# Stage-1 DFT of batches two to seven as float32r products, with inputs copied through a DRAM buffer

## Chip, cores and metric

The kernel runs on one core of a Trainium2 chip. The metric is the device time of one execution in microseconds. The engines are called by the profile's names: PE multiplies matrices, DVE, ACT and POOL (GpSimd) work on elements, and SP only issues DMAs here. Sixteen DMA engines carry the transfers of all queues.

## What is computed

A long convolution along the sequence (by a real FFT of 3008 points, a product with a filter, and the inverse), and behind it a two-layer network whose activation is a rational function:

```python
X = np.fft.rfft(x, axis=1)                    # x: (8, 3008, 256)
y = np.fft.irfft(X * F[None], n=3008, axis=1)
h = y.reshape(24064, 256) @ w_in              # (256, 2048)
P = a[0] + a[1]*h + a[2]*h**2 + a[3]*h**3
Q = 1.0 + abs(b[0])*abs(h) + abs(b[1])*h**2
out = (P / (Q + 1e-6)) @ w_out                # (2048, 256)
```

## The kernel before, in words

**The network.** The 24064 positions are cut into 47 tiles of 512, and each tile into 16 units of 128 hidden channels: 752 units. A unit has six matmuls into its hidden tile h_u (lines 459 to 462), five instructions on ACT, four on DVE and two on POOL, which give a number's upper part hi_u and lower part lo_u, and six matmuls of these with the second weights (lines 536 to 538). All twelve take float32r operands, a format that one matmul multiplies at once but that holds fewer bits than float32; three such products, upper by upper, lower by upper and upper by lower, stand for one product of float32 numbers.

**The convolution.** 3008 = 47 x 64. For each batch, stage 1 multiplies by the 47-point DFT matrix a1_sb (line 300), in eight quarters q of two products j each, 96 rows by 512 columns in float32. ACT evacuates a product to tile ev (names s1e), and one DMA per quarter stores it to DRAM (scr1). Tile ev has two buffers, so the evacuation of quarter q waits until the store of quarter q - 2 is done. Stage 2 loads it back in another order, multiplies by the 64-point DFT (products y, line 348), by the filter on DVE and POOL (lines 355 to 372), and by the inverse (products z, line 381), and stores to scr2. Stage 3 loads chunks tl of scr2, five columns at a time, and does the inverse 47-point DFT (products x, line 426), whose result is split into xh and xl, the network's input.

**Order.** Each engine takes its instructions in the order in which they are written. The function pipeline writes one unit per step i. Batch zero is done ahead of it; the other batches are a generator conv_items that the steps advance: it yields a cost in us of PE's time before each product, and a step takes one item when the saved credit (RATES, 0.6 per step for batch one, then 0.38) is above zero. A bare yield inside an item leaves its rest to a later place or step. Stage 1 has one bare yield per item, and so goes to the next item in the next step if the credit allows. Stage 3 takes precedence, and a chunk whose time has come before its batch is done runs the rest of the batch's generator at once (line 694).

The order of PE, ACT, DVE and POOL is that of the writing throughout. SP's is so only up to the first unit; after that the framework's scheduler places SP's DMAs, ahead of their place in the writing where nothing that they depend on holds them. Every DMA takes one of eight completion semaphores in turn and waits for the DMA that had it before.

Of the kernel before, what the change touches and what calls it, by code (L numbers as in the profile page):

```python
# [9 lines left out]
F32 = mybir.dt.float32  # L10
F32R = mybir.dt.float32r
I32 = mybir.dt.int32
U32 = mybir.dt.uint32
AF = mybir.ActivationFunctionType
ALU = mybir.AluOpType
# [9 lines left out]
NH = 32  # L25
K2 = 24
R1 = 96
C = 256
# [6 lines left out]
XF = 1  # L35
RING = dict(a=4, w=3, q=5, hi=5, lo=4)
GAP = 4
PGAP, XGAP = 1, 1
CPOS = 3
OG = 2  # L40
# [2 lines left out]
EV1, EV2, EVO = "A", "AV", "AV"  # L43
XB, FB = 4, 3
# [12 lines left out]
TT = 512  # L57
# [45 lines left out]
def conv_moe(ctx: ExitStack, tc: tile.TileContext, xp, fr, fi, w_in, w_out, ab, mats, small, sgn, outT):  # L103
    nc = tc.nc
    B = xp.shape[0]

    consts = ctx.enter_context(tc.tile_pool(name="consts", bufs=1))
    dram = ctx.enter_context(tc.tile_pool(name="dram", bufs=3, space=DRAM))
    conv = ctx.enter_context(tc.tile_pool(name="conv", bufs=2))
# [9 lines left out]
    xh = xl = None  # L119
    mats_sb = consts.tile([128, 3, 128], F32, name="mats_sb")  # L120
    small_sb = consts.tile([R1, R1 + GE], F32, name="small_sb")
    a1_sb, e_sb = small_sb[:, :R1], small_sb[:, R1 : R1 + G]
    words = consts.tile([128, 128], F32, name="words_sb")
    sgn_sb, ab_sb, abs_sb, cf_sb = words[:, :K2], words[:, 32:44], words[:, 64:76], words[:, 96:120]
    flag_sb = words[:, 120:121].bitcast(I32)
# [9 lines left out]
    def load_flag():  # L135


        nc.scalar.activation(abs_sb, ab_sb, AF.Abs)
        sq, c, d, e = col(8, 2), col(10, 2), col(12, 2), col(14)
        tt(out=sq, in0=ab_sb[:, 6:8], in1=ab_sb[:, 6:8], op=ALU.mult)  # L140
        tt(out=c, in0=abs_sb[:, 8:10], in1=abs_sb[:, 10:12], op=ALU.mult)
        stt(out=c, in0=c, scalar=16.0, in1=sq, op0=ALU.mult, op1=ALU.is_ge)
        stt(out=c, in0=abs_sb[:, 10:12], scalar=1e-6, in1=c, op0=ALU.is_ge, op1=ALU.mult)
        stt(out=d, in0=abs_sb[:, 10:12], scalar=2e-6, in1=abs_sb[:, 6:8], op0=ALU.mult, op1=ALU.is_le)
        tt(out=c, in0=c, in1=d, op=ALU.mult)

        stt(out=e, in0=B1, scalar=4.000004, in1=col(9), op0=ALU.mult, op1=ALU.subtract)
        tt(out=e, in0=e, in1=e, op=ALU.mult)
        tt(out=col(9), in0=col(9), in1=col(9), op=ALU.mult)
        stt(out=e, in0=col(9), scalar=1e-10, in1=e, op0=ALU.mult, op1=ALU.is_le)  # L150
        tt(out=col(10), in0=col(10), in1=e, op=ALU.mult)
        tt(out=flag_sb, in0=col(10), in1=col(11), op=ALU.mult)
# [42 lines left out]
    class Weights:  # L195
# [14 lines left out]
        def load(self):  # L210
            tag = ("oe", "tl", "oe", "tl", "raw")[self.i % 5] if self.i < HD else ("oe", "xin")[self.i % 2]
            raw = conv.tile([128, 2 * TT], I32, tag=tag, name=f"raw{self.i}", bufs={"xin": XB, "raw": 1}.get(tag))
            self.raw = raw.rearrange("p (n t) -> p n t", t=2)
            (nc.scalar if self.i < HD else nc.sync).dma_start(raw.rearrange("p (a c) -> p a c", a=2), self.src)
# [38 lines left out]
        return wo_sb[:, f // 2, k, c : c + 128]  # L253

    scr1 = [dram.tile([K2, 128, C], F32, tag="scr1", name=f"scr1_{b}") for b in range(B)]
    scr2 = [dram.tile([K2, 128, C], F32, tag="scr2", name=f"scr2_{b}") for b in range(B)]

    def rows(scr):
        return scr.rearrange("k (g m) c -> (k g) m c", m=NH)

    def evac(which, out, in_, i):
        if which[i % len(which)] == "A":
            nc.scalar.activation(out, in_, AF.Copy)  # L263
        else:
            nc.vector.tensor_copy(out, in_)
# [17 lines left out]
    def stage1_load(b, q):  # L283

        tag = "xin" if b or q < XB else ("f1", "f2")[q % 2]
        xin = conv.tile([R1, 2, TT], F32, tag=tag, name=f"xin{b}_{q}", bufs=XB if tag == "xin" else FB)
        nc.sync.dma_start(
            xin.rearrange("p a b -> p (a b)"), xp[b, :, 4 * q : 4 * q + 4, :].rearrange("p m c -> p (m c)")
        )
        return xin  # L290

    def stage1(b, q, xin=None):

        if xin is None:
            xin = stage1_load(b, q)
        ev = conv.tile([R1, 2, TT], F32, tag="ev", name=f"s1e{b}_{q}")
        for j in range(2):
            yield 0.86
            k, pt = banks.tile(f"s1_{b}_{q}_{j}")
            nc.tensor.matmul(pt[:R1], a1_sb, xin[:, j], start=True, stop=True)  # L300
            yield
            evac(EV1, ev[:, j], pt[:R1], 2 * q + j)
            banks.done(k, 0.5)
        nc.sync.dma_start(
            rows(scr1[b])[:, 4 * q : 4 * q + 4, :].rearrange("r m c -> r (m c)"), ev.rearrange("p a b -> p (a b)")
        )

    class Stage2:

# [81 lines left out]
    def stage2(b):  # L391
        s = Stage2(b)
        for q in range(2):
            s.load_filter(q)
            s.load(q)
        for i in range(13):
            if i < 12:
                yield from s.product(i)
            if i > 0:
                yield from s.inverse(i - 1)  # L400
            if i % 2 == 0 and i // 2 + 2 < 6:
                s.load_filter(i // 2 + 2)
                s.load(i // 2 + 2)
            if i > 0 and i % 2 == 0:
                s.store(i // 2 - 1)
# [134 lines left out]
    banks = None  # L540
# [12 lines left out]
    nt = B * S // T  # L553

    def conv_items(b):
        for q in range(8):
            yield from stage1(b, q)
        for _ in range(GAP):
            yield
        yield from stage2(b)  # L560

    def run(gen):
        for _ in gen:
            pass
# [3 lines left out]
    class Decode:  # L568
# [19 lines left out]
        def part(self, k):  # L588
            while self.parted < k:
                weights[self.parted].split()  # L590
                self.parted += 1
# [3 lines left out]
    def first_batch():  # L595

        s = Stage2(0)
        s.more = [xpool.tile([128, 6 - FB, 4, C], F32, tag=x, name=f"f{x}") for x in ("xh", "xl")]
        xin = {}
        fl = iter(range(6))  # L600

        def do(tokens):
            for c in tokens:
                if c == "W":
                    dec.load()
                elif c == "D":
                    dec.step()
                elif c == "F":
                    s.load_filter(next(fl))

        nc.scalar.dma_start(ab_sb, ab.rearrange("(o n) -> o n", o=1).broadcast_to([128, 12]))
        nc.sync.dma_start(small_sb, small)
        for q in range(8):
            xin[q] = stage1_load(0, q)
        do("W")
        nc.scalar.dma_start(sgn_sb, sgn)
        nc.scalar.dma_start(mats_sb, mats)
        load_flag()
        square_scalars()
        for q in range(8):  # L620
            run(stage1(0, q, xin.pop(q)))
            do(HA[q])
        for q in range(XB - 1):
            s.load(q)
        for q in range(2):
            s.double_filter(q)
        do(HM)
        for i in range(12 + ZL):
            if i < 12:
                run(s.product(i))  # L630
            if i >= ZL:
                run(s.inverse(i - ZL))
            q, j = divmod(i, 2)
            if j == 0 and q + XB - 1 < 6:
                s.load(q + XB - 1)
            elif j and q + 2 < 6:
                s.double_filter(q + 2)
            if i > ZL and (i - ZL) % 2:
                s.store((i - ZL) // 2)
            do(HB[i])  # L640
        nonlocal xh, xl
        xh, xl = (xpool.tile([128, 2, RX], F32R, tag=x, name=x) for x in ("xh", "xl"))
        for k in range(2):
            run(stage3(k))
        dec.part(HD)
        assert dec.done == dec.loaded == HD

    def pipeline(squares):
# [97 lines left out]
    with tc.manual_schedule(engines=ENGINES):  # L746
        banks = Banks(8 - T * 2 // TT)
        with tc.manual_schedule(engines=HEAD_SP):
            first_batch()
        free = dict(banks.free)  # L750

        def body(squares):
            dec.done = dec.loaded = dec.parted = HD
            banks.free = dict(free)
            pipeline(squares)

        if MODE == "if":
            flag = nc.values_load(flag_sb[:1, :1], min_val=0, max_val=1)
            with tc.If(flag > 0) as cmp:
                body(True)  # L760
            with cmp.Else():
                body(False)
        else:
            body(MODE == "squares")
# [53 lines left out]
```

## Time and profile before

| what | value |
|---|---|
| median of 3 runs | 2538.37 us (2537.87 to 2540.02) |
| the profiled execution | 2541.1 us, span 2538.9 us |
| mean granted clock of PE | 0.988 |
| DMA traffic | 208.76 MB in 102813 packets |
| stage-1 products (line 300) | 128, in the trace as 256 instructions |

Each figure of the profile is of this one execution. A float32 matmul stands in the trace as two instructions, a float32r one as one. A matmul's end is modelled and overlaps its successor's start, so the time that a matmul takes in a stream is read from start to start.

### The profile page before, as it was taken

To read this page: it belongs to the slowest core of one execution; us is meant where nothing else is said; L and a number is where in the kernel's file an instruction comes from. 1 tells how busy PE (TensorE), PEld (TensorE's weight loads), DVE (VectorE), ACT (ScalarE), POOL (GpSimd) and SP (SyncE) were. 2 spreads that over 40 slices of the span, in tenths; PEclk is the share of its full clock that TensorE was granted. 3 is DMA by queue.
4 is the path that set the end of the run, shared out by engine and by line. 5 is a ranking of instruction groups with operands and counts; after the bars stand their busy time and mean duration, and the time that the engine had idled before them with its cause. 6 is when DMAs were issued, how large, how long until landed. Compare 5 with 4: busy or idle time off the path is not lost.

```text
span 2538.9 us, 35897 instructions
## 1 busy us (share of the span) xinstructions
PE 2483.7 (98%) x10712; PEld 1935.9 (76%) x10712; DVE 2263.7 (89%) x3549; ACT 2199.2 (87%) x4170; POOL 1856.3 (73%) x1984
## 2 busy tenths in 40 slices
PE   5799999999999999999999999999999999999998
PEld 1477777777777777777777777777777778888887
DVE  5779988999889998899888998899988999999998
ACT  4588889888988889888998889988898889999997
POOL 3558876788668876788668886688767887677676
PEclk8799999999999999999999999999999999999999
DMA  8653331332223231232223232233323210000000
GB/s 255 190 140 100 102 116 54 107 97 86 73 76 102 83 97 54 83 110 88 75 60 109 86 97 73 69 97 95 89 62 95 70 52 28 25 25 17 25 9 19
DMA packets 102813, 208.76 MB, mean 82 GB/s; under 512 B 8752, under 2 KB 58512, under 8 KB 102608
## 3 DMA queue, kind: packets, MB, share of 16 engines
q1 hardware_dynamic: 99536, 199.34, 26.6%
q10 hardware_dynamic: 3072, 7.03, 0.9%
q8 instruction: 87, 1.43, 0.2%
q14 instruction: 118, 0.97, 0.1%
HBM read 131.36 MB, written 74.97 MB: 81 GB/s over the span
## 4 chain that ended last, share of the span: by engine, by line
PE 94%; DMA 2%; DVE 2%; ACT 2%; issue 0%; SPq 0%; ACTq 0%; DVEq 0%
PE o L536 13%; PE o L537 13%; PE o L538 13%; PE h_u L459 13%; PE h_u L460 13%; PE h_u L462 13%; PE x L426 4%; PE s L300 4%; PE y L348 3%; PE z L381 3%; DMA scr<-s1e 1%; DMA f<-fi 0%; DMA fxl<-fi 0%; DMA xin<-xp 0%; ACT s1e L263 0%
## 5 line engine op out<-in xcount | busy, mean ns | idle before, releaser
L518 POOL TENSOR_TENSOR q_u<-q_u,hi_u 128x512 f32<-128x512 f32 x752 | 974.5, 1296 | 490.5 <-DVE hi_u L513 472.6
L536 PE MATMUL o<-hi_u,wo_sb 128*128 128x512 f32 x1504 | 701.2, 466 | 0.0
L467 ACT ACTIVATE q_u<-h_u 128x512 f32<-128x512 f32 x752 | 450.3, 599 | 201.3 <-PE h_u L462 144.5
L513 DVE SCALAR_TENSOR_TENSOR hi_u<-h_u,words_sb,a_u 128x512 fp32r<-128x512 f32 x752 | 561.1, 746 | 61.9 <-ACT a_u L489 59.2
L521 DVE SCALAR_TENSOR_TENSOR h_u<-h_u,words_sb,q_u 128x512 f32<-128x512 f32 x752 | 566.5, 753 | 53.8 <-POOL q_u L518 53.4
L459 PE MATMUL h_u<-xh,wi_sb 128*128 128x512 f32 x1504 | 596.9, 397 | 3.7 <-DVE xl L437 3.7
L537 PE MATMUL o<-lo_u,wo_sb 128*128 128x512 f32 x1504 | 589.4, 392 | 0.3 <-DVE lo_u L527 0.3
L538 PE MATMUL o<-hi_u,wo_sb 128*128 128x512 f32 x1504 | 589.1, 392 | 0.0
L460 PE MATMUL h_u<-xl,wi_sb 128*128 128x512 f32 x1504 | 588.2, 391 | 0.0
L499 POOL TENSOR_SCALAR q_u<-q_u,words_sb 128x512 f32<-128x512 f32 x752 | 583.6, 776 | 3.6 <-ACT a_u L484 3.6
L504 DVE SCALAR_TENSOR_TENSOR h_u<-w_u,words_sb,h_u 128x512 f32<-128x512 f32 x752 | 562.7, 748 | 4.3 <-ACT w_u L474 4.3
L527 DVE TENSOR_TENSOR lo_u<-h_u,a_u 128x512 fp32r<-128x512 f32 x752 | 515.8, 686 | 0.1
L484 ACT ACTIVATE a_u<-q_u 128x512 f32<-128x512 f32 x752 | 475.6, 632 | 0.1
L489 ACT ACTIVATE a_u<-a_u 128x512 f32<-128x512 f32 x752 | 471.2, 627 | 0.0
L480 ACT ACTIVATE q_u<-q_u 128x512 f32<-128x512 f32 x752 | 469.6, 624 | 0.0
L462 PE MATMUL h_u<-xh,wi_sb 128*128 128x512 f32 x1504 | 465.2, 391 | 0.0
L474 ACT ACTIVATE w_u<-h_u 128x512 f32<-128x512 f32 x752 | 444.1, 591 | 0.0
L536 PEld LDWEIGHTS o<-hi_u,wo_sb 128*128 128x128 f32 x1504 | 283.1, 188 | 112.9 <-issue 63.6
L537 PEld LDWEIGHTS o<-lo_u,wo_sb 128*128 128x128 f32 x1504 | 283.2, 188 | 110.2 <-issue 60.1
L459 PEld LDWEIGHTS h_u<-xh,wi_sb 128*128 128x128 f32 x1504 | 283.5, 189 | 72.3 <-DVE lo_u L527 4.7
L460 PEld LDWEIGHTS h_u<-xl,wi_sb 128*128 128x128 f32 x1504 | 283.6, 189 | 64.8 <-issue 4.1
L538 PEld LDWEIGHTS o<-hi_u,wo_sb 128*128 128x128 f32 x1504 | 282.5, 188 | 62.2
(96 smaller groups left out, 1889.9 us busy)
## 6 DMA issues: line engine op xcount, KB each, us to landing
xin<-xp SPq DMA_DIRECT2D x64, 384.0 KB, 3.9
scr<-s1e SPq DMA_DIRECT2D x64, 384.0 KB, 4.1
xin<-scr SPq DMA_DIRECT2D x48, 512.0 KB, 4.9
scr<-ev SPq DMA_DIRECT2D x48, 512.0 KB, 4.6
outT<-oe SPq DMA_DIRECT2D x47, 512.0 KB, 3.3
f<-fr SPq DMA_DIRECT2D x87, 256.0 KB, 4.1
f<-fi SPq DMA_DIRECT2D x87, 256.0 KB, 3.8
tl<-scr SPq DMA_DIRECT2D x44, 480.0 KB, 4.1
```

The source lines that it names most:

```text
L459: nc.tensor.matmul(o, w_in_part(0, f, cc), xh[:, cc, ts], start=cc == 0, stop=False)
L460: nc.tensor.matmul(o, w_in_part(0, f, cc), xl[:, cc, ts], start=False, stop=False)
L462: nc.tensor.matmul(o, w_in_part(1, f, cc), xh[:, cc, ts], start=False, stop=cc == 1)
L499: nc.gpsimd.tensor_scalar(out=self.q, in0=self.q, scalar1=AIK, scalar2=SGN, op0=ALU.mult, op1=ALU.add)
L504: v.scalar_tensor_tensor(out=H, in0=w, scalar=PK, in1=H, op0=ALU.add, op1=ALU.mult)
L513: nc.vector.scalar_tensor_tensor(out=self.hi, in0=self.H, scalar=self.p0, in1=self.a, op0=ALU.add, op1=ALU.mult)
L518: nc.gpsimd.tensor_tensor(out=self.q, in0=self.q, in1=self.hi.bitcast(F32), op=ALU.mult)
L521: nc.vector.scalar_tensor_tensor(out=self.H, in0=self.H, scalar=self.p0, in1=self.q, op0=ALU.add, op1=ALU.subtract)
L527: nc.vector.tensor_tensor(out=self.lo, in0=self.H, in1=self.a, op=ALU.mult)
L536: nc.tensor.matmul(o, w_out_part(0, f, dd), self.hi, start=f == 0, stop=False)
L537: nc.tensor.matmul(o, w_out_part(0, f, dd), self.lo, start=False, stop=False)
L538: nc.tensor.matmul(o, w_out_part(1, f, dd), self.hi, start=False, stop=f == 15)
```

## The change

Batches two to seven (three to eight, counted from one) get a new stage 1, stage1_parts; zero and one keep the old. A quarter's input is copied from the kernel's input xp to a DRAM tile scr0 (copy), and loaded from there to xin (load). For each of the two halves, ACT copies it to float32r, the upper part (tile xh), and POOL subtracts that from the input, in place, for the lower part, one bare yield later. Three float32r matmuls with the two parts of the matrix (a1r_sb, made once) take the place of the float32 one. The item's cost is 0.69 instead of 0.86. The generator yields three times at its start (PART), and each item has a second bare yield.

```diff
+PART = 3
+    a1r_sb = consts.tile([R1, 2, R1], F32R, name="a1r_sb")
+    scr0 = [None] + [dram.tile([R1, NH, C], F32, tag="scr0", name=f"scr0_{b}", bufs=2) for b in range(1, B)]
+    def stage1_parts(b):
+        xin, his = {}, {}
+        def copy(q):
+            m = slice(4 * q, 4 * q + 4)
+            nc.sync.dma_start(scr0[b][:, m], xp[b, :, m])
+        def load(q):
+            xin[q] = conv.tile([R1, 2, TT], F32R, tag="xin", name=f"xin{b}_{q}", bufs=XB)
+            src = scr0[b][:, 4 * q : 4 * q + 4].rearrange("p m c -> p (m c)")
+            nc.sync.dma_start(xin[q].bitcast(F32).rearrange("p a b -> p (a b)"), src)
+        def part(i):
+            q, j = divmod(i, 2)
+            if j == 0:
+                his[q] = conv.tile([R1, 2, TT], F32R, tag="raw", name=f"xh{b}_{q}", bufs=1)
+            x, hi = xin[q][:, j], his[q][:, j]
+            nc.scalar.activation(hi, x.bitcast(F32), AF.Copy)
+            yield
+            nc.gpsimd.tensor_tensor(out=x, in0=x.bitcast(F32), in1=hi.bitcast(F32), op=ALU.subtract)
+        for q in range(3):
+            copy(q)
+        load(0)
+        load(1)
+        yield 0.1
+        for _ in range(PART):
+            yield
+        yield from part(0)
+        for i in range(16):
+            q, j = divmod(i, 2)
+            if j == 0:
+                ev = conv.tile([R1, 2, TT], F32, tag="ev", name=f"s1e{b}_{q}")
+                if q + 3 < 8:
+                    copy(q + 3)
+                if q + 2 < 8:
+                    load(q + 2)
+            yield 0.69
+            k, pt = banks.tile(f"s1_{b}_{q}_{j}")
+            hi, lo = his[q][:, j], xin[q][:, j]
+            nc.tensor.matmul(pt[:R1], a1r_sb[:, 0], hi, start=True, stop=False)
+            nc.tensor.matmul(pt[:R1], a1r_sb[:, 0], lo, start=False, stop=False)
+            nc.tensor.matmul(pt[:R1], a1r_sb[:, 1], hi, start=False, stop=True)
+            yield
+            evac(EV1, ev[:, j], pt[:R1], i)
+            banks.done(k, 0.5)
+            if i < 15:
+                yield from part(i + 1)
+            if j:
+                m = slice(4 * q, 4 * q + 4)
+                nc.sync.dma_start(rows(scr1[b])[:, m, :].rearrange("r m c -> r (m c)"), ev.rearrange("p a b -> p (a b)"))
     def conv_items(b):
-        for q in range(8):
-            yield from stage1(b, q)
+        if b > 1:
+            yield from stage1_parts(b)
+        else:
+            for q in range(8):
+                yield from stage1(b, q)
...
         dec.part(HD)
+        nc.scalar.activation(a1r_sb[:, 0], a1_sb, AF.Copy)
+        nc.gpsimd.tensor_tensor(out=a1r_sb[:, 1], in0=a1_sb, in1=a1r_sb[:, 0].bitcast(F32), op=ALU.subtract)
```

SP's queue, from the load of chunk tl3 (just after the first units) to the store of batch one's first stage-1 quarter, before. xin1_2 is the input of batch one's quarter 2, f11_0 a filter tile.

```order
L420 DMA tl3_977<-scr2_0_88 96x1280
L287 DMA xin1_2_890<-xp 96x1024
L420 DMA tl4_1257<-scr2_0_88 96x1280
L325 DMA f11_0_1570<-fr 64x1024 x2
L287 DMA xin1_3_958<-xp 96x1024
L304 DMA scr1_1_81<-s1e1_0_687 96x1024
```

The same stretch of SP's queue in the changed kernel, where scr0_b is the copy of batch b:

```order
L477 DMA tl3_987<-scr2_0_96 96x1280
L317 DMA scr0_2_90<-xp 96x1024 x8
L317 DMA scr0_3_91<-xp 96x1024 x8
L317 DMA scr0_4_92<-xp 96x1024
L290 DMA xin1_2_900<-xp 96x1024
L317 DMA scr0_4_92<-xp 96x1024 x7
L317 DMA scr0_5_93<-xp 96x1024 x2
L477 DMA tl4_1267<-scr2_0_96 96x1280
L382 DMA f11_0_1580<-fr 64x1024 x2
L317 DMA scr0_5_93<-xp 96x1024 x4
L290 DMA xin1_3_968<-xp 96x1024
L307 DMA scr1_1_82<-s1e1_0_697 96x1024
```

Thirty copies, of batches two to five, stand ahead of that store; four more stand between it and the second store (s1e1_1), and the last fourteen between that and the third, which these rows of SP's queue show:

```order
L307 DMA scr1_1_82<-s1e1_1_831 96x1024
L382 DMA f11_2_1664<-fr 64x1024
L382 DMA f21_2_1665<-fi 64x1024 x2
L317 DMA scr0_6_94<-xp 96x1024 x6
L317 DMA scr0_7_95<-xp 96x1024 x8
L290 DMA xin1_6_1248<-xp 96x1024
L307 DMA scr1_1_82<-s1e1_2_902 96x1024
```

So all 48 copies stand in the queue before the third store of batch one, none at the batch that uses it.

On PE, the end of batch five's stage 2 before, where the last product z_5_11 stands in unit 423 and the first chunk that needs the batch (x_32) in unit 434:

```order
L459 MATMUL h_u423_15130<-xh_603,wi_sb_75 128x512
L460 MATMUL h_u423_15130<-xl_604,wi_sb_75 128x512
L462 MATMUL h_u423_15130<-xh_603,wi_sb_75 128x512 x2
L381 MATMUL z_5_11_15137<-f15_5_14294,mats_sb_77 128x512
L536 MATMUL o26_0_15099<-hi_u418_15038,wo_sb_76 128x512
```

The same place on PE in the changed kernel (y and z are stage 2's products, tl32 is chunk 32):

```order
L519 MATMUL h_u441_15969<-xh_611,wi_sb_75 128x512 x2
L438 MATMUL z_5_9_15977<-f15_4_15138,mats_sb_77 128x512
L405 MATMUL y_5_11_15981<-xin5_5_15436,mats_sb_77 128x512
L438 MATMUL z_5_10_15992<-f15_5_15430,mats_sb_77 128x512
L438 MATMUL z_5_11_15995<-f15_5_15430,mats_sb_77 128x512
L593 MATMUL o27_0_15872<-hi_u436_15886,wo_sb_76 128x512
...
L519 MATMUL h_u442_16024<-xh_611,wi_sb_75 128x512 x2
L483 MATMUL x_32_0_16031<-small_sb_78,tl32_15999 128x94 x5
```

Four products of the batch stand together in unit 441, and x_32 follows one unit later. In the same way z_2_11 moved from unit 151 to 160 with x_13 at 162 in both, and z_4_11 from 332 to 352 with x_26 at 354 in both.

## Prediction

> **What bounds the kernel now.** I read the busy table, the slices and the chain of waits first, then stretches of 300 us, then the timeline of single units.
>
> ```profile
> PE 2483.7 (98%) x10712; PEld 1935.9 (76%) x10712; DVE 2263.7 (89%) x3549; ACT 2199.2 (87%) x4170; POOL 1856.3 (73%) x1984
> PE 94%; DMA 2%; DVE 2%; ACT 2%; issue 0%; SPq 0%; ACTq 0%; DVEq 0%
> 1000.00:1300.00 300.00, 299.75 (x1302) 233.86 (x1301) 269.79 (x419) 264.43 (x503) 224.92 (x243) 1.00 0.28 84
> ```
>
> PE is busy in 299.75 of 300 us, the chain that ended last runs through PE for 94% of the span, and its clock there is 1.00. DVE (270) and ACT (264) have a tenth left. Busy PE might hide gaps, so I look at one place where each unit starts (its first L459):
>
> ```profile
> 1002.67 0.39 PE L459 MATMUL h_u<-xh,wi_sb 128*128 128x512 f32 x1
> 1004.03 1.02 PE L300 MATMUL s<-xin,small_sb 96*96 96x512 f32 x2
> 1006.28 0.39 PE L459 MATMUL h_u<-xh,wi_sb 128*128 128x512 f32 x1
> 1009.00 0.39 PE L459 MATMUL h_u<-xh,wi_sb 128*128 128x512 f32 x1
> ```
>
> The second unit takes 2.72 us for its 12 float32r matmuls, 0.227 us each, back to back. The first has one stage-1 product in it and takes 3.61, so a float32 product costs 0.89. PE is the bound from about 130 us on: what leaves PE there is gained, and what makes PE wait there is lost.
>
> **The product itself.** Batches two to seven, counted from zero as the names are, have 96 such products. Each 0.89 becomes three float32r matmuls, 3 x 0.227 = 0.68: 0.21 x 96 = **20 us gained**. That 96 rows stream like 128 isn't shown; if they brought nothing the term would be 0.
>
> **ACT and GpSimd.** Each item gains a float32r copy on ACT and a subtraction on POOL, and now takes two units, since its generator yields once more.
>
> ```profile
> 2406.46 0.65 ACT L489 ACTIVATE a_u<-a_u 128x512 f32<-128x512 f32 x1
> 2408.50 0.63 ACT L467 ACTIVATE q_u<-h_u 128x512 f32<-128x512 f32 x1
> 2408.98 0.67 ACT L489 ACTIVATE a_u<-a_u 128x512 f32<-128x512 f32 x1
> L518 POOL TENSOR_TENSOR q_u<-q_u,hi_u 128x512 f32<-128x512 f32 x752 | 974.5, 1296 | 490.5 <-DVE hi_u L513 472.6
> L499 POOL TENSOR_SCALAR q_u<-q_u,words_sb 128x512 f32<-128x512 f32 x752 | 583.6, 776 | 3.6 <-ACT a_u L484 3.6
> 160.39 0.60 ACT L263 ACTIVATE s1e<-s 96x512 f32<-96x512 f32 x1 [0.20 <-PE s L300]
> ```
>
> A unit's five ACT instructions pass in 2.52 us (2406.46 to 2408.98), one in 0.48. Two units with one item: PE 2 x 2.72 + 0.68 = 6.12, ACT 2 x 2.52 + 2 x 0.48 = 6.00, POOL 2 x 2.07 + 1.30 = 5.44. So 96 copies (46 us) and 96 subtractions (125 us) lie beside PE's work, the copies with 0.12 us per item to spare. If the evacuation's 0.20 us wait for PE stays, ACT needs 6.20 and the cover is gone: 0.08 x 96 = 8 us. I take 0, as ACT may lag PE and then doesn't wait. The two a1r_sb instructions are one each (under 1 us), and the load has the 384 KB it had.
>
> **The DRAM copies.** Written inside the generator, up to three quarters ahead of use, they don't stay there: SP's order isn't fixed by hand after the first unit, and the order shows all 48 of them, of all six batches, between tl3's load and the third s1e store of batch one. What stands there before:
>
> ```profile
> 103.07 0.36 SPq L420 DMA_DIRECT2D tl<-scr  x1
> 126.83 0.32 SPq L304 DMA_DIRECT2D scr<-s1e  x1
> 136.06 0.37 SPq L304 DMA_DIRECT2D scr<-s1e  x1
> 142.44 0.32 SPq L304 DMA_DIRECT2D scr<-s1e  x1
> 105.00:110.00 5.00, 4.35 (x12) 2.65 (x11) 2.08 (x3) 4.32 (x7) 1.40 (x2) 0.69 0.94 227
> 110.00:115.00 5.00, 2.23 (x15) 1.85 (x14) 2.44 (x4) 5.00 (x11) 0.20 (x1) 0.99 0.01 4
> 130.00:135.00 5.00, 5.00 (x20) 3.38 (x19) 4.10 (x7) 4.23 (x8) 4.92 (x5) 1.00 1.04 235
> 135.00:140.00 5.00, 5.00 (x22) 3.73 (x21) 4.59 (x8) 4.62 (x10) 4.22 (x5) 1.00 1.04 247
> 60.00:65.00 5.00, 4.56 (x11) 2.20 (x12) 4.76 (x8) 3.66 (x5) 3.69 (x7) 1.00 1.04 312
> xin<-xp SPq DMA_DIRECT2D x64, 384.0 KB, 3.9
> scr<-s1e SPq DMA_DIRECT2D x64, 384.0 KB, 4.1
> f<-fr SPq DMA_DIRECT2D x87, 256.0 KB, 4.1
> fxh<-fr SPq DMA_DIRECT2D x3, 256.0 KB, 7.7
> tl<-scr SPq DMA_DIRECT2D x44, 480.0 KB, 4.1
> ```
>
> The stores were issued at 126.83, 136.06 and 142.44. Now 30, 34 and 48 copies stand ahead of them, and SP issues each DMA only when the eighth before it is done, so it can't run far ahead of the transfers. DMAs on one queue share the rate: the same 256 KB land in 4.1 us alone, in 7.7 where the share is full. The older work is through at 110 (share 0.94, then 0.01). Up to the third store come 48 x 384 KB = 18.87 MB of copies, and five xin loads, three stores, twelve filter halves and tl4, 6.78 MB: 25.66 MB. No DRAM-to-DRAM transfer is in this trace. The nearest rows are 130 to 140, where 4 KB rows as of the copies fill the queue: 235 and 247, mean 241 GB/s. So the third store lands at 110 + 25.66 MB / 241 GB/s = 110 + 106.5 = 216.5.
>
> Who waits: tile ev has two buffers, so s1e of quarter 4 needs the third store done. Its evacuation is the L263 at 160.39 above. ACT then stands until 216.5, with every ACT instruction of the units queued behind it, and DVE, POOL and PE follow within some two units. **56 us lost**; the first and second stores cause parts of the same delay and don't add. PE was full there, so nothing makes it up. Best case, the 312 GB/s of 60 to 65: 82.2 us, 192.2, 32 lost. Worst, a copy paying its read and its write at 241 each (120.5): 156.6 + 28.1 = 184.7, so 134 lost. I take 56, of the rows nearest in kind.
>
> The Trainium skill, "DMA: Bandwidth & Descriptors", section "Latency and other measured facts", gives 207 to 214 GB/s for copies between HBM tensors at moderate pitch; no run here shows it yet. By 214 the copies would take 88.2 us and the loss would be 66. The same page of the Trainium skill, section "Queues, rings and completion order", has each DMA engine take descriptors in ring order, and the 7.7 us against 4.1 agrees.
>
> **The later calendar.** Items of two units make stage 1 longer (batch five's last z product in unit 441, was 423), so some stage-3 chunks meet their data.
>
> ```profile
> scr<-ev SPq DMA_DIRECT2D x48, 512.0 KB, 4.6
> tl<-scr SPq DMA_DIRECT2D x3, 96.0 KB, 1.9
> tl<-scr SPq DMA_DIRECT2D x3, 192.0 KB, 2.4
> L355 DVE TENSOR_TENSOR f<-y,f 128x512 f32<-128x512 f32 x90 | 61.6, 685 | 14.7 <-PE y L348 14.1
> L367 POOL TENSOR_SCALAR zw<-f,words_sb 64x256 f32<-64x256 f32 x336 | 157.3, 479 | 114.6 <-DVE f L355 50.7 <-issue 42.6 <-POOL q_u L499 13.4
> L372 POOL TENSOR_TENSOR f<-f,zw 128x512 f32<-128x512 f32 x84 | 108.3, 1289 | 0.0
> ```
>
> In unit 441 the rest of batch five is emitted at once. After y_5_11, z_5_11 needs two DVE products (2 x 0.69) and five POOL instructions (4 x 0.48 + 1.29), 4.6 us, against one z product of 0.89: 3.7 waited. Then x_32 needs evacuation 0.69, store 4.6 and load 1.9, 7.2 us, against one unit of PE work, 2.7: 4.5 waited. Chunks 13 and 26 come two units after their batch's last z (160 to 162, 352 to 354): 0.69 + 4.6 + 2.4 = 7.7 us against 5.4, 2.3 each. Sum 8 + 5 = **13 us lost**, from 0 (if PE lags its helpers by as much) to twice that, 26.
>
> **Sum.** 2541.1 - 20 + 56 + 13 = 2590.1 for the profiled execution (span 2538.9 and 2.2 around it). The median shown is 2.7 lower, 2538.4: **2587**. By the rate of the Trainium skill's page it would be 2597.
>
> **Rivals.**
> - *The copies are hidden* and the time falls: 2538.4 - 20 + 13 = 2531. For it: the queue was idle at 110 to 115, and the s1e stores need 384 KB each. It decides if the third store lands no later than 160.4 plus the 7 us that the other terms leave: 25.66 MB in 57 us, 450 GB/s. The best full stretch above has 312. 5%.
> - *A copy pays twice*, read and write at full price: 134 lost, 2538.4 - 20 + 134 + 13 = 2665. Against it: a load too reads one memory and writes another, at one price. 10%.
> - *ACT becomes the bound in stage 1* (6.20 against 6.12): 8 more, 2595. The margin is thin, but the lag of four units lets it even out. 7%.
> - *The float32r product is no cheaper* at 96 rows, so the change doesn't do what it says: 2607. The 0.227 holds over the twelve matmuls of a unit, with four different moving operands. 3%.
> - My forecast, 2587 by itself from 2550 (312 GB/s, no calendar loss: 2538.4 - 20 + 32) to 2620: 75%.
>
> The range 2550 to 2630 takes in the forecast, the third and fourth cases and copies down to 156 GB/s (18.87 MB in 121 us, 99 lost); it leaves out the first two, 15%. A difference under 0.2% (5 us) can't be told from no change. Slower: 93%; faster, from the first rival alone: 5%; between: 2%.
>
> **What would show it.** Right: a new group of 48 DMAs near 105 to 215 us, DMA share near 1 for a hundred us, ACT's L263 of batch one waiting on DMA scr<-s1e for about 55 us in sum, PE idle there, PE back at 2.72 a unit behind it, and units with a stage-1 product at 3.40. The calendar shows as PE idle by L426 waiting for tl near chunks 13, 26 and 32. Wrong: stores landing near 145, or landing of a copy so quick that L263 never waits, or ACT idle nowhere and PE waiting on lo_u in stage 1.

## The result, and the profile after

| | median | runs |
|---|---|---|
| before | 2538.82 us | 2537.87 to 2540.02 |
| after | 2575.68 us | 2573.71 to 2578.07 |
| ratio | 1.014 | 95% interval 1.0128 to 1.0153 |

The change makes the kernel 37 us slower. The forecast was 2587, its range 2550 to 2630. The profiled execution after has a span of 2576.2 us, 37.3 more than before.

The busy table of after, and its slices of PE and of the DMA engines:

```profile
PE 2479.5 (96%) x10808; PEld 1958.6 (76%) x10808; DVE 2260.5 (88%) x3549; ACT 2223.6 (86%) x4267; POOL 1977.6 (77%) x2081
PE   4769999999999999999999998999999999999998
DMA  8893332232222323233222233213322231110000
```

PE's busy time is almost what it was and its share fell by two points. The slices (64 us each) say where: the third PE digit, 129 to 193 us, is a 6, and the DMA digit below it is a 9.

SP's timeline of after there, cut to one load of tl, the copies and the stores (start, duration, line, transfer, count):

```profile
105.41 0.36 SPq L477 DMA_DIRECT2D tl<-scr  x1
105.81 19.30 SPq L317 DMA_DIRECT2D scr<-xp  x17
126.96 10.13 SPq L317 DMA_DIRECT2D scr<-xp  x9
142.50 3.08 SPq L317 DMA_DIRECT2D scr<-xp  x4
147.76 0.32 SPq L307 DMA_DIRECT2D scr<-s1e  x1
155.73 5.14 SPq L317 DMA_DIRECT2D scr<-xp  x4
162.88 0.38 SPq L307 DMA_DIRECT2D scr<-s1e  x1
166.22 15.08 SPq L317 DMA_DIRECT2D scr<-xp  x14
183.06 0.32 SPq L307 DMA_DIRECT2D scr<-s1e  x1
```

All 48 copies (L317) are issued between 105.81 and 181.3. Batch one's first three s1e stores stand behind 30, 34 and 48 of them and leave at 147.76, 162.88 and 183.06, where they left at 126.83, 136.06 and 142.44 before. ACT's timeline of after shows who waited; these are the evacuations that found no free buffer:

```profile
155.80 0.59 ACT L266 ACTIVATE s1e<-s 96x512 f32<-96x512 f32 x1 [16.70 <-DMA scr<-s1e]
170.90 0.59 ACT L266 ACTIVATE s1e<-s 96x512 f32<-96x512 f32 x1 [6.94 <-DMA scr<-s1e]
192.28 0.59 ACT L266 ACTIVATE s1e<-s 96x512 f32<-96x512 f32 x1 [6.14 <-DMA scr<-s1e]
```

The last of them is the first evacuation of quarter 4, which was at 160.39 before: 31.9 us later, of which 29.8 (16.70 + 6.94 + 6.14) are waits for stores. The rest is a lag of about two us that was there ahead of the first copy: SP issues the load of tl just before it at 105.41, and did so at 103.07 before. Where that lag comes from wasn't settled. Three stretches of after over the copies (PE, PEld, DVE, ACT, POOL busy with counts; then PE's clock, DMA share, GB/s):

```profile
140.00:150.00 10.00, 2.01 (x9) 1.31 (x7) 0.64 (x2) 0.00 (x0) 1.07 (x2) 0.78 1.01 341
150.00:160.00 10.00, 3.55 (x7) 2.08 (x8) 2.71 (x5) 4.20 (x9) 2.05 (x2) 0.50 1.04 251
180.00:190.00 10.00, 9.04 (x37) 6.32 (x35) 7.39 (x12) 5.53 (x11) 4.13 (x5) 1.00 1.02 348
```

The DMA engines are full (1.00 to 1.04 in all eight stretches of ten us from 110 to 190), and but for one stretch they move 329 to 352 GB/s, some 340, not the 241 of the forecast. The one with 251 is the one over which SP issued filter halves: six between 148.4 and 155.2. ACT does nothing from 140 to 150.

PE's timeline of after at the place where 2.72 and 3.61 us were read before, cut to the units' first matmuls and the new product:

```profile
1004.53 0.39 PE L516 MATMUL h_u<-xh,wi_sb 128*128 128x512 f32 x1
...
1005.89 0.40 PE L353 MATMUL s<-xh,a1r_sb 96*96 96x512 f32 x1
1006.13 0.40 PE L354 MATMUL s<-xin,a1r_sb 96*96 96x512 f32 x1
1006.37 0.39 PE L355 MATMUL s<-xh,a1r_sb 96*96 96x512 f32 x1
1006.59 0.39 PE L593 MATMUL o<-hi_u,wo_sb 128*128 128x512 f32 x1
...
1007.96 0.39 PE L516 MATMUL h_u<-xh,wi_sb 128*128 128x512 f32 x1
...
1010.68 0.39 PE L516 MATMUL h_u<-xh,wi_sb 128*128 128x512 f32 x1
```

A unit without a product still takes 2.72 us (1007.96 to 1010.68), one with a product 3.43 (1004.53 to 1007.96), 0.18 less than before. The three matmuls take 0.24, 0.24 and 0.22 from start to start.

Last, the rows of PE's timeline after 260 us in which PE stood still at the places that the forecast named, and the stretches behind them:

```profile
680.74 0.68 PE L483 MATMUL x<-small_sb,tl 96*128 96x94 f32 x4 [2.23 <-DMA tl<-scr]
1304.23 1.59 PE L483 MATMUL x<-small_sb,tl 96*128 96x94 f32 x6 [3.24 <-DMA tl<-scr]
1590.39 1.13 PE L438 MATMUL z<-f,mats_sb 128*128 128x512 f32 x2 [1.76 <-POOL f L429]
1593.81 2.07 PE L438 MATMUL z<-f,mats_sb 128*128 128x512 f32 x2 [2.28 <-POOL f L429]
1596.10 0.63 PE L594 MATMUL o<-lo_u,wo_sb 128*128 128x512 f32 x1
1596.53 0.63 PE L595 MATMUL o<-hi_u,wo_sb 128*128 128x512 f32 x1
1604.60 0.74 PE L483 MATMUL x<-small_sb,tl 96*128 96x94 f32 x2 [3.25 <-DMA tl<-scr]
```

```profile
681.00:684.00 3.00, 3.00 (x11) 2.40 (x11) 1.89 (x4) 2.54 (x6) 0.00 (x0) 0.60 0.26 73
1304.00:1308.00 4.00, 3.77 (x12) 3.29 (x13) 1.48 (x4) 2.14 (x6) 0.00 (x0) 0.50 0.22 58
1594.00:1600.00 6.00, 6.00 (x13) 4.06 (x14) 3.92 (x6) 1.20 (x3) 2.06 (x3) 0.52 0.90 206
1605.00:1610.00 5.00, 5.00 (x14) 3.94 (x14) 3.22 (x5) 2.60 (x5) 0.66 (x1) 0.50 0.05 13
```

Chunks 13 (680.74), 26 (1304.23) and 32 (1604.60) wait for their data, and between them stands unit 441 with its two z products that wait for POOL. The idle times sum to 12.8 us. But behind these stops stands a second price: PE reads as busy, at a granted clock of 0.50 to 0.60 for three to six us, and the matmuls at 1596.10 and 1596.53 start 0.43 us apart, not 0.227. Busy time times the missing clock is 3.00 x 0.40 + 3.77 x 0.50 + 6.00 x 0.48 + 5.00 x 0.50 = 8.5 us in these four stretches. So the calendar cost about 21 us by this estimate.

The account: 32 (copies, with the lag of two) + 21 (calendar) - 17 (0.18 x 96 products) = 36, of 37.3 in the span.

### The profile page after: what moved, and what is told of

It reads as the page before. It is cut to its first block, busy times and chain, and to the rows that moved or that the text cites. A ratio compares the mean times of both kernels' runs of the same rounds, so it can differ in the third digit from the quotient of the medians.

```text
span 2576.2 us, 36441 instructions
## 1 busy us (share of the span) xinstructions
PE 2479.5 (96%) x10808; PEld 1958.6 (76%) x10808; DVE 2260.5 (88%) x3549; ACT 2223.6 (86%) x4267; POOL 1977.6 (77%) x2081
## 4 chain that ended last, share of the span: by engine, by line
PE 89%; DMA 5%; DVE 2%; ACT 1%; issue 1%; POOL 1%; SPq 0%; ACTq 0%; DVEq 0%; POOLq 0%
PE o L593 13%; PE o L595 13%; PE o L594 13%; PE h_u L516 13%; PE h_u L517 13%; PE h_u L519 12%; PE x L483 4%; PE y L405 3%; PE z L438 3%; DMA scr<-xp 2%; DMA scr<-s1e 1%; PE s L353 1%; PE s L354 1%; PE s L355 1%; DMA scr<-ev 1%
## 5 line engine op out<-in xcount | busy, mean ns | idle before, releaser
L593 PE MATMUL o<-hi_u,wo_sb 128*128 128x512 f32 x1504 | 667.1, 444 | 0.0
L595 PE MATMUL o<-hi_u,wo_sb 128*128 128x512 f32 x1504 | 591.8, 394 | 0.0
```

The costliest lines, as they stand in the source:

```text
L593: nc.tensor.matmul(o, w_out_part(0, f, dd), self.hi, start=f == 0, stop=False)
L595: nc.tensor.matmul(o, w_out_part(1, f, dd), self.hi, start=False, stop=f == 15)
```

## Experiments

The theory after the result: the copies cost by their place in SP's queue, through batch one's s1e stores; the calendar and its clock cost some 20; the product gains some 17. Rivals: the copies cost by their traffic wherever they stand; ACT or POOL, with more work in stage 1, set a part of the time; the calendar's stops only move work.

**e1: no copies.** The input is loaded straight from xp into a float32 tile and the lower part goes to a tile of its own; the rest is the changed kernel.

```diff
-            nc.sync.dma_start(scr0[b][:, m], xp[b, :, m])
...
-            src = scr0[b][:, 4 * q : 4 * q + 4].rearrange("p m c -> p (m c)")
+            src = xp[b, :, 4 * q : 4 * q + 4, :].rearrange("p m c -> p (m c)")
...
+            lo = los[i] = conv.tile([R1, TT], F32R, tag="zw", name=f"lo{b}_{i}")
+            nc.gpsimd.tensor_tensor(out=lo, in0=x, in1=hi.bitcast(F32), op=ALU.subtract)
```

> Stage 1 by parts as in the change, but without the DRAM copies: the input is loaded straight from xp, and the lower part goes to a tile of its own. My ledger of the changed kernel (2575.7) against the one before (2538.8) is: copies +31, late stage-3 chunks +23, cheaper products -17. If it holds, the copies' 31 go and all else stays: 2545 (2541 to 2549), with no wait of ACT's s1e evacuations for their stores in batch one, and PE still idle at chunks 13, 26 and 32. Rival 1 (the stall at 140 to 200 us comes from something else than the copies): 2576. Rival 2 (the idle at the chunks comes from the copies' and loads' places in SP's queue, not from the pace of the items): both go, 2522.

Measured: 2542.60 us (2540.49 to 2546.20), 1.0014 of before (1.0005 to 1.0024). Without the copies 33 of the 37 us are gone. The same places of PE's timeline in e1 still stop, by 13.1 us in sum:

```profile
647.94 0.68 PE L483 MATMUL x<-small_sb,tl 96*128 96x94 f32 x4 [2.25 <-DMA tl<-scr]
1269.64 0.91 PE L483 MATMUL x<-small_sb,tl 96*128 96x94 f32 x6 [3.11 <-DMA tl<-scr]
1554.79 1.12 PE L438 MATMUL z<-f,mats_sb 128*128 128x512 f32 x2 [1.74 <-POOL f L429]
1558.20 2.07 PE L438 MATMUL z<-f,mats_sb 128*128 128x512 f32 x2 [2.28 <-POOL f L429]
1568.02 0.74 PE L483 MATMUL x<-small_sb,tl 96*128 96x94 f32 x2 [3.67 <-DMA tl<-scr]
```

So the calendar's loss doesn't come from the copies, and in e1 it eats what the product gains. Not every stop has the second price here: behind the first one the matmuls stand 0.24 us apart at once (648.72 and 648.96), with a granted clock of 1.00 from 648 to 651. In sum over stretches of four us from 250 to 2050, PE's idle time and the clock missing from its busy time are 17.4 us in e1 (13.0 and 4.4) and 22.2 in after (12.7 and 9.5).

**e2: the copies alone.** The kernel before, with its float32 products, and the 48 copies and loads from them.

```diff
+        src = scr0[b] if b > 1 else xp[b]
...
         for q in range(8):
+            if b > 1:
+                for n in range(3) if q == 0 else (q + 2,):
+                    if n < 8:
+                        nc.sync.dma_start(scr0[b][:, 4 * n : 4 * n + 4], xp[b, :, 4 * n : 4 * n + 4])
             yield from stage1(b, q)
```

> The kernel before with its float32 products and its pace, but with the inputs of batches two to seven copied through the DRAM buffer; SP's queue then has 48 copies ahead of batch one's third stage-1 store, as in the changed kernel. If the copies in the queue are the cause: 2538.8 + 30 = 2569 (2565 to 2573), all of it lost before 200 us. Rival (the parts on ACT and GpSimd, or the changed stage 1, cause the early loss): 2539.

Measured: 2568.55 us, 1.0115 of before (1.0098 to 1.0132), 29 us of the medians and 25.8 of the spans (2564.7 against 2538.9). ACT's timeline of e2 has the same three waits as after:

```profile
151.45 0.59 ACT L264 ACTIVATE s1e<-s 96x512 f32<-96x512 f32 x1 [14.55 <-DMA scr<-s1e]
165.52 0.59 ACT L264 ACTIVATE s1e<-s 96x512 f32<-96x512 f32 x1 [6.22 <-DMA scr<-s1e]
186.31 0.59 ACT L264 ACTIVATE s1e<-s 96x512 f32<-96x512 f32 x1 [5.40 <-DMA scr<-s1e]
```

26.2 us of waiting, and 25.8 us lost by the spans or 29 by the medians. With e1 this shows the copies' loss from both sides: they cost it without any of the change's arithmetic. The 33 between e1 and after are 4 more than the 29 here. The waits in after are 3.6 longer, its load of tl ahead of the first copy stands 3.6 later than in e1 (101.83), and PE's idle time and missing clock differ by 4.8; how these share the 4 us wasn't settled.

**e3: an earlier calendar, copies kept.** The changed kernel without the three yields at the generator's start, and with two in place of four ahead of stage 2, for all batches.

```diff
-GAP = 4
-PART = 3
+GAP = 2
+PART = 0
```

> The changed kernel with PART 0 for 3 and GAP 2 for 4, so that a batch takes five steps less: in the written order the last z product of batches two, four and five then stands 11, 27 and 14 units ahead of the first chunk that needs the batch (changed: 2, 2 and 1). If the pace is the cause of PE's idle time there (23 us): 2575.7 - 23 = 2553 (2549 to 2557). Rival (the copies or loads in SP's queue delay the chunks' loads): 2576. The early loss of 31 us stays in both.

Measured: 2562.79 us, 1.0087 of before (1.0071 to 1.0104): 13 us better than after, not 23. The forecast missed, and PE's timeline of e3 has a stop that after doesn't have:

```profile
375.12 2.02 PE L483 MATMUL x<-small_sb,tl 96*128 96x94 f32 x8 [4.05 <-DMA tl<-scr]
```

GAP holds for batch one too. Its last z moved from unit 66 to 64, the chunk that waits for batch one to be done moved from 75 to 66, and that is too close. The later stops were gone. With the slow clock behind it (0.50 from 374 to 378) the new stop is worth 6.5 us by the stretches. That leaves 3 to 4 us of the miss open. So an edit that clears three places of a calendar opened a fourth; e5 tests that reading.

**e4: half of the copies.** Batches two to four use scr0, five to seven load from xp; the lower part in a tile of its own as in e1.

```diff
+            if b < 5:
+                nc.sync.dma_start(scr0[b][:, m], xp[b, :, m])
...
+            src = (scr0[b] if b < 5 else xp[b])[:, 4 * q : 4 * q + 4].rearrange("p m c -> p (m c)")
```

> The changed kernel with the DRAM buffer for batches two to four only (24 copies); five to seven load from xp, with the lower part in a tile of its own everywhere. The queue works at some 335 GB/s in the changed kernel's trace. Up to batch one's first store there are then 24 copies and 2.2 MB more, 11.6 MB, 35 us from 112: landed at 147, where its evacuation would come at 140.5: 7 us late; the third store, 16.2 MB, at 160 where 162.7 would do. So, if the delay is a queue with slack, 2545 + 7 = 2552 (2549 to 2556). Rival (each copy costs its share, 31/48 of a us): 2545 + 15.5 = 2560.

Measured: 2559.46 us (2555.85 to 2561.89), 1.0073 of before (1.0057 to 1.009): 17 us above e1, where 48 copies cost 33. The forecast of 2552 missed, and the rival's 2560 was near. ACT's timeline of e4:

```profile
150.22 0.59 ACT L266 ACTIVATE s1e<-s 96x512 f32<-96x512 f32 x1 [11.58 <-DMA scr<-s1e]
162.70 0.59 ACT L266 ACTIVATE s1e<-s 96x512 f32<-96x512 f32 x1 [4.95 <-DMA scr<-s1e]
```

The third store no longer holds anything, but the first does: all 24 copies stand ahead of it, as 30 did in after, and its wait is 11.58 where it was 16.70. 11.58 + 4.95 = 16.5, the measured 17. So by these rows what counts is each store, with the bytes that stand ahead of it, and not the last one alone. The time itself fits the rival too, a fixed price of some 0.7 us per copy; e8 tells the two apart.

**e5: no copies, and the calendar clear.** e1 without the three yields, with two ahead of stage 2 from batch two on, and four for batch one as before. The last z of batches two to five stand in units 153, 244, 329 and 420, their chunks in 162, 258, 354 and 434.

```diff
-PART = 3
+PART = 0
...
-        for _ in range(GAP):
+        for _ in range(GAP if b < 2 else 2):
```

> No copies (the input is loaded straight from xp to a float32 tile, the lower part goes to a tile of its own, as in e1_no_copies), and the calendar moved: PART 0, GAP 2 for batches two to seven, GAP 4 for batch one as it was, so that its last z stands in unit 66 and chunk 7 in 74 again, not in 64 and 66, where e3_shorter_calendar lost 6 us. The last z of each batch stands 9 to 30 units ahead of the first chunk that needs it. Theory (the three calendar places are all that e1 still loses): e1's 2542.6 less its 17 us of late starts there, 2525 (2521 to 2530). Rival (the products only move, and ACT, with 0.12 us to spare in two units, sets the pace in stage 1 when items follow closely): 2535 to 2543.

Measured: 2524.88 us (2523.67 to 2526.54), 0.994 of before (0.9926 to 0.9953): faster than both kernels. Against e1 that is 17.7 us for the calendar, more than the 13.1 us of idle time shown in e1, and near the 17.4 of idle time and missing clock; in PE's timeline of e5 the places of e1 have no idle row any more. Its stretch that answers to the first one shown of before:

```profile
1000.00:1300.00 300.00, 300.00 (x1339) 239.84 (x1338) 269.30 (x421) 271.85 (x527) 248.39 (x263) 1.00 0.29 86
```

PE never stops, at full clock, with ACT at 272 of 300 and POOL at 248 (264 and 225 before): ACT's and POOL's new work lies beside PE's, and the rival that has ACT set the pace falls.

**e6 and e7: the copies at their place.** The changed kernel, the copies issued on ACT's or POOL's queue, whose order is that of the writing.

```diff
-            nc.sync.dma_start(scr0[b][:, m], xp[b, :, m])
+            nc.scalar.dma_start(scr0[b][:, m], xp[b, :, m])
```

(e7 has gpsimd where e6 has scalar.)

> The changed kernel with one word changed: the 48 copies are issued on ACT's queue, whose order is that of the writing, so each stands at the item that it was written in, and none is ahead of batch one's stores. Theory (the 32 us are the place of the copies in SP's queue, not their traffic): 2543, as e1_no_copies, and up to 17 more for ACT's 48 issues (at most 0.35 us each, as SP's rows show for an issue), so 2543 to 2560. Rival (the copies cost by their traffic wherever they stand): 2576.

> As e6, but on POOL's queue, which has 0.3 us a unit to spare. Theory: 2543 to 2555. Rival (traffic): 2576. If POOL's issues are long (over 1 us each) stage 1 becomes POOL's: the time would then be above 2560 and POOL's busy time or its waits in stage 1 would show it.

Measured: e6 2555.90 us, 1.0061 of before (1.0046 to 1.0077); e7 2560.51 us, 1.0076 (1.0061 to 1.0092). The same bytes through the same copies, and 20 and 15 us of the 33 are back. What stays is another wait. The row of the copy's line in e6 (least, median and longest time of an issue in ns; first and last start), and the wait of ACT's L330 (us, times), first in e6, then in e7:

```profile
L317 ACTq DMA_DIRECT2D scr<-xp x48: 497/498/1201, 338.1 to 1962.3; - x48
  DMA xin<-scr: 13.5, 6
```

```profile
  DMA xin<-scr: 18.1, 5
```

At a batch's start the first load is written right behind its copy, three yields ahead of the first item, and the two in a row take too long: ACT waits for the input, each time at the first item of a batch. In after this wait is absent, since all copies were long done. An issue costs 0.50 us on ACT (the expectation said at most 0.35) and, by the median, 0.56 on POOL. e7's 2560 is above the 2555 that its expectation gave the theory. Against e1, PE's idle time and missing clock from 250 to 2050 are 10.0 us more in e6 and 14.7 in e7, of the 13.3 and 17.9 lost by the medians; the remainder was not taken apart. That traffic costs wherever it stands (2576) falls.

**e8: twice the copies.** Each copy is issued a second time, into a DRAM tile that nothing reads.

```diff
             nc.sync.dma_start(scr0[b][:, m], xp[b, :, m])
+            nc.sync.dma_start(scr00[b][:, m], xp[b, :, m])
```

> Each copy is issued twice, the second into a DRAM tile that nothing reads: 96 copies. They stand in SP's queue 30, 34, 59, 88 and 96 ahead of the first five s1e stores of batch one. Theory (a store lands when the bytes ahead of it have passed at the 335 GB/s that the changed kernel showed, from 110 us): the fourth store, with 43.2 MB, lands at 239 to 245, and quarter 5's evacuation, which needs it, stood at 167.6 before: 71 to 80 us lost, so 2542.6 + 75 = 2618 (2610 to 2628). Rival (a price of 0.7 us per copy, 33 us for 48, whatever stands behind): 2609. Rival (241 GB/s as put in the prediction): 289, 121 lost, 2664.

Measured: 2617.84 us (2615.72 to 2618.96), 1.0303 of before (1.0287 to 1.0319), on the forecast of 2618 and away from 2609 and 2664. ACT's timeline of e8, and a stretch of it:

```profile
154.27 0.59 ACT L267 ACTIVATE s1e<-s 96x512 f32<-96x512 f32 x1 [15.81 <-DMA scr<-s1e]
170.83 0.59 ACT L267 ACTIVATE s1e<-s 96x512 f32<-96x512 f32 x1 [9.22 <-DMA scr<-s1e]
205.22 0.59 ACT L267 ACTIVATE s1e<-s 96x512 f32<-96x512 f32 x1 [19.10 <-DMA scr<-s1e]
241.46 0.59 ACT L267 ACTIVATE s1e<-s 96x512 f32<-96x512 f32 x1 [28.79 <-DMA scr<-s1e]
251.23 0.59 ACT L267 ACTIVATE s1e<-s 96x512 f32<-96x512 f32 x1 [1.73 <-DMA scr<-s1e]
```

```profile
200.00:240.00 40.00, 9.71 (x28) 6.41 (x28) 5.33 (x8) 6.24 (x12) 4.09 (x4) 0.63 1.00 352
```

The waits sum to 74.7 us, and the loss against e1 is 75.2. The longest belongs to quarter 5, at 241.46; it needs the fourth store, that of quarter 3, which was forecast to land at 239 to 245. Per copy the loss is 0.78 us, where it was 0.69 for 48 copies and 0.70 for 24, so a fixed price isn't far off, but it misses by 9 us and the bytes ahead of the stores, at the 335 GB/s of the expectation, give the time.

## Why the prediction was right, step by step

- **Mechanism and verdict: right.** The 48 copies stood where the order had them, the stores landed late, ACT's evacuation of quarter 4 waited with everything behind it, and nothing made it up. e2 shows the loss without the rest of the change, e1 the rest without the loss, e6 that the place in the queue makes at least 20 of the 33 us.
- **Copies, 56 us: the size was off, 32 measured.** The step that failed is the choice of 241 GB/s, from the rows 130 to 140 of before "where 4 KB rows as of the copies fill the queue". Those 10 us held mostly something else. Of the ten DMAs issued in them before, eight are 256 KB filter halves (transfer, count, size, us to landing):

```profile
f<-fi SPq DMA_DIRECT2D x5, 256.0 KB, 8.0
f<-fr SPq DMA_DIRECT2D x3, 256.0 KB, 8.4
```

The copies moved some 340 GB/s. The halves end in 64 partitions of a tile and the copies in DRAM; which difference makes the rate, no run separates. The row set aside as the best case, 312 GB/s, gives 192.2 us and 32 lost; measured were 192.28 and 31.9. That they meet so closely is luck: the eight stretches from 110 to 190 have 331 in the mean, and about two us of the 31.9 are the lag ahead of the copies. The waits for the first two stores are parts of the delay that the third one ends, as the prediction had it; with other places (e4) it is the first that makes most of it.
- The Trainium skill, "DMA: Bandwidth & Descriptors", section "Latency and other measured facts", gives 207 to 214 GB/s for copies between HBM tensors of 128 rows of 16 KiB, 207 at a row pitch of 512 KiB and 214 at 4 MiB padded by 4 KiB. The copies here have 96 rows of 4 KB, 32 KB apart. By 214 the loss would have been 66 us, an estimate; the trace has some 340 in the stretches above, and the measurement decides.
- **The calendar, 13 us: the places and the idle time were right, the price was not; some 20 measured.** The idle times are 2.23 and 3.24 for chunks 13 and 26 (2.3 each was put) and 1.76 + 2.28 + 3.25 = 7.3 for unit 441 and chunk 32 (8.2 was put): 12.8. The missing part of the term is PE's clock behind the stops, which the prediction put at nothing; it is worth 8.5 by the stretches. That the loss is real and not a displacement is shown by e5: 17.7 us came back against e1, where the stops carried less of the slow clock.
- The Trainium skill, "TensorE: Matmul & The Clock Gate", section "Part 1: The HAM clock gate (the "warmup" mystery)", has the array at half rate after an idle window of about 3.4 us until it has been busy about as long. The half rate (0.50, 0.43 us a matmul) agrees; here 2.23 us of idle time by the profile were enough for 0.60 over the next 3 us, and in e1 2.25 us were not.
- **The product, 20 us: about 17 measured.** A unit with a product fell from 3.61 to 3.43, not 3.40, as two of the three matmuls take 0.24 instead of 0.227. e5 against before is 17.1 us by the spans and 15.4 by the medians.
- **ACT's and POOL's new work, 0: right.** e5's stretch has PE at 300.00 of 300.
- The errors partly cancel: 24 us too much loss for the copies, 8 too little for the calendar, 3 too much gain, 24 - 8 - 3 = 13, and the forecast was 11 too high. That it came so near is in part luck. The rival in which the copies are hidden fell with the first store's wait; the one in which a copy pays twice, with the 340 GB/s.

## What to carry to other kernels

A DMA that depends on nothing may be issued much earlier than it is written, and then delays every store behind it on its queue: read the queue's order before you price a transfer, and price it by the bytes ahead of the first store that an engine waits for. Take a rate from a stretch that is filled with the same transfers, not only with the same packets. When an edit stretches one stage, look at every later place where another stage meets its data, and price a stop of PE with the slow clock that can follow it; removing the copies and moving the calendar turned a loss of 1.4% into a gain of 0.6%.

## What the runs showed of the hardware

Copies from DRAM to DRAM went through the shared queue at 329 to 352 GB/s in stretches that held mostly copies, above the 235 to 247 of a stretch of loads of filter halves before and the 251 of such a stretch in after, with the DMA engines equally full (1.00 to 1.04). And most stops of PE of two to three us were followed by three to six us at a granted clock near 0.5: in after, 12.8 us of idle time cost about 21 by the stretches, and in e1, where one stop of 2.25 us had full clock behind it, 13.1 us of idle time cost 17.7.
